# Reordering the attention work on VectorE, the loads of the last stage and the end of the block in a fused attention and gated-FFN kernel

## The chip, the cores and the metric

The kernel runs on one core of one Trainium2 chip. The metric is device time in microseconds (us) of one execution; lower is better.

## What is computed

`x` is layer-normalised once; the result feeds a local dilated attention (A) and a gated feed-forward network (B), and the output is `x + A * silu(B)`. There are 2048 tokens, 1024 features, 32 heads of 32, a window of 8 keys at a distance of 2, and 3584 hidden features.

```python
def reference(A_x, A_wqkv, A_wo, B_x, B_w1, B_w3, B_w2):
    xn = _layernorm(A_x)
    # attention: every query sees the keys at s, s-2, ..., s-14
    q, k, v = split(xn @ A_wqkv)                       # 32 heads of 32
    logits = einsum("bhsd,bhswd->bhsw", q, kg) * 32 ** -0.5
    attn = softmax(where(mask, logits, -1e9))
    s = einsum("bhsw,bhswd->bhsd", attn, vg) @ A_wo
    # gated FFN
    h = silu(xn @ B_w1) * (xn @ B_w3)
    g = silu(h @ B_w2)
    return A_x + s * g
```

## The kernel before

One function, `build`, writes a list of operations for each engine; an operation waits for those it depends on. Each engine, and each queue that issues transfers (SP's and POOL's), runs its list strictly in order. Four stages follow each other on TensorE (PE):

- **Normalisation and the first projection** (0 to about 45 us): rows are normalised on VectorE (DVE) and transposed on PE.
- **QKV projection** (to about 191 us): the 1024 features are cut into eight groups `g` of 128 (four heads). For each group and each of 16 row tiles PE makes 8 matmuls of 384 columns (L447), ScalarE (ACT) copies the result out and SP writes it to DRAM (`k_qkv_scr`). POOL's queue meanwhile loads the FFN's weights w3 and w1 (`k_w_sb`), a piece every four row tiles.
- **FFN** (to about 820 us): tokens are cut into eight blocks `b` of 256. An item S1(k) is 16 matmuls of 256 columns (L997) for one of 28 slices of hidden features; ACT then writes a sigmoid to `k_s_ring` (L1010) and a copy to `k_gu_ring` (L1012). Four items make a batch: two multiplications on DVE (L854, L855), `Hb_a` and `dH`. The ring holds 12 items, so ACT's L1010 of item k waits for the batch of item k-12. An item S3(k) is four matmuls of 512 columns (L1045), which need the batch of k and one 256 KB tile of w2. Segment `s` runs S1 of block s interleaved with S3 of block s-1: three S1 first, then pairs of one S3 and one S1, then three S3. Segment 0 has S1 only, segment 8 has S3 only. At the end of a segment ACT empties the accumulators (L1066 `aT2`, L1068 `aT2c`), POOL multiplies (L863, `dG`) and stores the gate `g` to DRAM (`gst`).
- **Final stage F** (to the end): for each of 16 row tiles the attention output is loaded (SP, `k_Or`), transposed on PE (L931, `pT`), multiplied with `wo` (L947, `pS`); DVE multiplies with `g` and adds `x` (L954, L956; their loads `k_gF` and `k_xF` come from POOL's queue), and POOL's queue stores the output.

The **attention** itself is done on DVE, in the gaps of its FFN work. For each group: **L**, eight steps of a product of q and k and a reduction (L561, L563); **S1**, mask, maximum and subtraction (three operations, to L583); the exponential `aE` on ACT; **S2**, sum, reciprocal and scaling (L603 to L605); **AV**, two halves of 8 steps (L623, L627, L629), each half followed by a store of `k_prod` to `k_O_scr` from POOL's queue (`Ost`). There is one buffer `k_prod`: the next L or AV half may start only when the store before it has landed. Q, K and V have one buffer each: loads for group g+1 are issued (POOL's queue) when the L, or the AV, of group g is done. `Er`, the output of `aE`, has two buffers, so `aE` of group g needs AV of group g-2.

What sets DVE's order is a planner in `build` that keeps estimated clocks for PE and DVE (`pe_clock`, `st["dv"]`). `advance_dve` picks, at each point of PE's list, the earlier of the next FFN batch and the next step of a fixed attention list `att_steps`: L(0), S1(0), L(1), S1(1), S2(0), AV(0), L(2), S1(2), S2(1), AV(1), and so on. The first two exponentials are put on ACT's list only where the FFN begins.

In segment 8 the w2 tiles go through six buffers, `w2r` (three), `w2tA` (two) and `w2tB` (one): tile k+6 is requested when S3(k) is done. Into SP's list between those requests the code puts one piece of `wo` at each even f from 2 and one load of the attention output at each odd f from 3, the latter with the two POOL loads of `g` and `x` (`F_loadgx`); one `pT` stands at f = 12, 16, 20 and 24.

```python
    with nc.Block() as block:                      # L98
...
    att_steps.append(("S2", g, 0, 0))              # L640, after L and S1 of group g+1
...
                if f >= 3 and f % 2 == 1 and ldO_left and F_can_loadO(ldO_left[0]):   # L976
```

## Time and profile before

| | us |
|---|---|
| median of 4 runs | 900.51 (897.93 to 904.2) |
| the profiled execution, its own time | 899.81 |
| span of its trace, first to last instruction | 898.0 |
| PE busy in the span | 836.5 |
| DVE busy | 631.1 |
| ACT busy | 329.1 |
| mean granted clock of PE | 0.975 of full |

The span and what lies around it (1.8 us) make the execution's own time. A busy figure is the time in which an engine has an instruction under way; matmuls overlap, so PE can be busy without running at its best rate. An idle time before an instruction carries a releaser: what ended it. Under `PEclk` stands the share of its full clock that PE was granted. Row numbers such as L997 are lines of the kernel before.

### The profile page before, as it was taken

The page shows a single profiled execution, that of the slowest core. Times are in us where ns is not written, and L with a number is a line of the kernel's source. Part 1 is how long each engine was busy: PE and PEld are TensorE (multiplying, and loading weights), DVE is VectorE, ACT ScalarE, POOL GpSimd, SP SyncE. Part 2 cuts the span into 40 slices and gives each one's busy share as a digit, 9 for nine tenths or more (in the row PEclk, how much of TensorE's full clock was granted, in tenths as well). Part 3 has the DMA queues.
Part 4 walks back from the last instruction along what each step waited for, and adds up shares of the span by engine and source line. Part 5 has one row for each costly group of instructions (what it writes and reads, how often), then busy time and mean ns, then how long its engine had stood idle before and what let it go on. Part 6 is the DMA issues. An engine that isn't in the chain of part 4 may idle for free.

```text
span 898.0 us, 14107 instructions
## 1 busy us (share of the span) xinstructions
PE 836.5 (93%) x5943; PEld 582.8 (65%) x6016; DVE 631.1 (70%) x624; ACT 329.1 (37%) x646; POOL 124.8 (14%) x170
## 2 busy tenths in 40 slices
PE   4999999999999999999998999899979999868995
PEld 3656665678877777777776776667657777523552
DVE  7558750047899879779978997997899797400553
ACT  3723233355533443453442343234224432402220
POOL 4322010000000020020002000100200020222341
PEclk9999999999999999999999899999989999978998
DMA  8288999730235465454545244454523454595772
GB/s 256 66 293 263 328 300 320 223 113 12 80 102 166 119 197 165 119 173 137 163 140 173 77 167 134 156 162 133 169 71 95 118 178 113 157 367 197 249 230 90
DMA packets 96176, 152.00 MB, mean 169 GB/s; under 512 B 32752, under 2 KB 52208, under 8 KB 96112
## 3 DMA queue, kind: packets, MB, share of 16 engines
q1 hardware_dynamic: 83072, 91.84, 34.3%
q0 software_dynamic: 13040, 59.25, 19.5%
q8 instruction: 47, 0.77, 0.3%
q14 instruction: 17, 0.14, 0.1%
HBM read 122.16 MB, written 28.90 MB: 168 GB/s over the span
## 4 chain that ended last, share of the span: by engine, by line
DVE 41%; PE 38%; DMA 10%; issue 7%; SPq 2%; ACT 1%; POOL 0%; DVEq 0%; POOLq 0%; ACTq 0%
PE k_ps L447 15%; DVE k_prod L627 11%; PE k_ps L997 9%; DVE k_Lr L563 7%; PE k_ps L1045 7%; DVE k_prod L561 7%; PE k_ps L947 6%; DVE k_prod L629 5%; DMA k_O_scr<-k_prod 5%; DVE k_s_ring L854 3%; DVE k_h_ring L855 3%; DMA k_qkv_scr<-k_ev 3%; SPq L84 2%; DMA k_w2tB<-in_B_w_dram 1%; DVE k_prod L623 1%
## 5 line engine op out<-in xcount | busy, mean ns | idle before, releaser
L997 PE MATMUL k_ps<-k_xblkB,k_w_sb 128*128 128x256 bf16 x1792 | 214.2, 274 | 5.8 <-ACT k_gu_ring L1012 5.8
L1010 ACT ACTIVATE k_s_ring<-k_ps 128x256 bf16<-128x256 f32 x224 | 88.1, 393 | 342.6 <-DVE k_h_ring L855 188.0
L1045 PE MATMUL k_ps<-k_w2r,k_h_ring 128*128 128x512 bf16 x781 | 203.2, 385 | 7.5 <-ACT k_accb L1068 3.8
L997 PEld LDWEIGHTS k_ps<-k_xblkB,k_w_sb 128*128 128x128 bf16 x1792 | 175.8, 98 | 49.8 <-ACT k_gu_ring L1012 8.0
L447 PE MATMUL k_ps<-k_wq,k_xnT_full 128*128 128x384 bf16 x1024 | 170.7, 328 | 5.8 <-DMA k_wq<-in_A_wqkv_dram 3.1
L997 PE MATMUL k_ps<-k_xblkA,k_w_sb 128*128 128x256 bf16 x1344 | 163.0, 276 | 12.0 <-ACT k_gu_ring L1012 12.0
L997 PEld LDWEIGHTS k_ps<-k_xblkA,k_w_sb 128*128 128x128 bf16 x1344 | 132.8, 99 | 46.7 <-ACT k_gu_ring L1012 14.0
L563 DVE TENSOR_REDUCE k_Lr<-k_prod 128x64 f32<-128x2048 bf16 x64 | 146.4, 2288 | 2.2
L447 PEld LDWEIGHTS k_ps<-k_wq,k_xnT_full 128*128 128x128 bf16 x1024 | 99.8, 98 | 71.7 <-issue 4.7
L627 DVE TENSOR_TENSOR k_prod<-k_Vb,k_Er 128x1024 bf16<-128x1024 bf16 x112 | 137.0, 1223 | 2.9
L1012 ACT ACTIVATE k_gu_ring<-k_ps 128x512 bf16<-128x512 f32 x224 | 136.2, 608 | 0.0
L1045 PEld LDWEIGHTS k_ps<-k_w2r,k_h_ring 128*128 128x128 bf16 x844 | 83.2, 99 | 67.4 <-issue 8.9
L561 DVE TENSOR_TENSOR k_prod<-k_Qb,k_Kb 128x2048 bf16<-128x2048 bf16 x64 | 87.4, 1365 | 50.7 <-DMA k_Kb<-k_qkv_scr 28.0
L453 ACT ACTIVATE k_ev<-k_ps 128x384 bf16<-128x384 f32 x128 | 57.8, 499 | 108.4 <-PE k_ps L447 54.6
L629 DVE TENSOR_TENSOR k_prod<-k_prod 128x1024 bf16<-128x1024 bf16 x112 | 77.5, 692 | 3.8
L954 DVE TENSOR_TENSOR k_gF<-k_ps,k_gF 128x1024 bf16<-128x1024 f32 x16 | 19.6, 1225 | 81.3 <-PE k_ps L947 81.3
L84 POOL DMA_DIRECT2D k_O_scr<-k_prod x16 | 14.5, 906 | 400.4 <-DVE k_prod L629 326.2
L947 PE MATMUL k_ps<-k_wo_sb,k_OTr 128*128 128x512 bf16 x249 | 59.7, 393 | 4.1 <-ACT k_accb L1068 3.7
L603 DVE TENSOR_REDUCE k_ss<-k_Er 128x64 f32<-128x512 bf16 x8 | 5.4, 679 | 67.8 <-ACT k_Er L590 67.8
L997 PE MATMUL k_ps<-k_xnT_full,k_w_sb 128*128 128x256 bf16 x448 | 49.1, 273 | 0.0
L997 PEld LDWEIGHTS k_ps<-k_xnT_full,k_w_sb 128*128 128x128 bf16 x448 | 43.8, 98 | 5.2
L947 PEld LDWEIGHTS k_ps<-k_wo_sb,k_OTr 128*128 128x128 bf16 x256 | 25.2, 101 | 33.5 <-ACT k_accb L1068 4.2
(51 smaller groups left out, 425.0 us busy)
## 6 DMA issues: line engine op xcount, KB each, us to landing
k_w2r<-in_B_w_dram SPq DMA_DIRECT2D x211, 256.0 KB, 2.6
k_w_sb<-in_B_w_dram POOLq DMA_DIRECT2D x16, 896.0 KB, 6.7
k_qkv_scr<-k_ev SPq DMA_DIRECT2D x32, 384.0 KB, 4.9
k_Kb<-k_qkv_scr POOLq DMA_DIRECT2D x8, 960.0 KB, 6.7
k_Vb<-k_qkv_scr POOLq DMA_DIRECT2D x8, 960.0 KB, 6.5
k_wq<-in_A_wqkv_dram SPq DMA_DIRECT2D x64, 96.0 KB, 5.3
k_x_in<-in_A_x_dram SPq DMA_DIRECT2D x8, 512.0 KB, 6.8
k_Qb<-k_qkv_scr POOLq DMA_DIRECT2D x8, 512.0 KB, 4.4
```

What stands on the lines that cost most here:

```text
L84: op.fns = [lambda e, o=out_ap, i=in_ap: e.dma_start(o, i)]
L447: fns = [lambda e, kt=kt, t=t, pos=pos, bk=bk: e.matmul(bank(bk, 0, NQ), lhsT=xnT_full[:, t // TB, kt, (t % TB) * P:(t % TB + 1) * P], rhs ...
L453: op_acB[idx] = AC.add(lambda e, idx=idx, bk=bk, pr=pr, t=t: e.activation(ev_ring[pr % 2][:, :, t % EVT_, :], bank(bk, 0, NQ).rearrange("p ...
L561: m = DV.add(lambda e, ksl=ksl: e.tensor_tensor(prodb[:], Qb[:], Kb[:, ksl:ksl + NT, :], ALU.mult), deps=deps, key=("Lm", g, w))
L563: last = DV.add(lambda e, w=w, g=g: e.tensor_reduce(Lview(Lr[0], w), prodb[:].rearrange("p t (h d) -> p (t h) d", d=DH), AX.X, ALU.add), d ...
L627: m = DV.add(lambda e, Vv=Vv, Pw=Pw: e.tensor_tensor(tmp, Vv, Pw, ALU.mult), deps=[AV_last[(g, hh)]], key=("AVm", g, hh, w))
L629: last = DV.add(lambda e: e.tensor_tensor(acc, acc, tmp, ALU.add), deps=[m], key=("AVa", g, hh, w))
L947: fns.append(lambda e, kt=kt, half=half, sl=sl, so=so: e.matmul(bank(4 + sl * ND + half, 0, 512), lhsT=OTr[so][:, kt, :], rhs=wo_sb[:, kt, ...
L997: fns.append(lambda e, kt=kt, f=f, b=b, k=k, which=which, wsb=wsb: e.matmul(bank(k % 4, which * NCOL, (which + 1) * NCOL), lhsT=wsb[:, kt, ...
L1010: AC.add(lambda e, k=k, sl=sl: e.activation(t_ring[:, sl, :], bank(k % 4, 0, NCOL), ACT.Sigmoid), deps=deps, key=("aS1t", k))
L1012: op_aS1[k] = AC.add(lambda e, k=k, sl=sl: e.activation(gu_ring[:, sl, :], bank(k % 4, 0, 2 * NCOL), ACT.Copy), deps=[op_pS1[k]], key=("aS ...
L1045: fns.append(lambda e, sub=sub, half=half, slot=slot, k=k, f=f, wbuf=wbuf: e.matmul(bank(4 + sub * ND + half, 0, 512), lhsT=h_ring[:, slot ...
```

## The change

Four things are changed.

1. The block is made with `no_gpsimd_drain=True`.
2. The one list of attention steps becomes two: `ls_steps` (L and S1) and `av_steps` (S2 and AV). At each point the planner may take the next step of either, whichever it estimates to start first (AV on a tie), but does not interrupt a group's L or AV. An L may start when S1 of the group before is in the list; four `Dr` buffers (`NDR`) bound how far L may run ahead of `aE`. The estimate also knows of the store of `k_prod` now (`ready_prod`, the end of the AV half plus 4.5 us).
3. `aE` of a group is put into ACT's list only when AV of the group two before stands in DVE's list, ahead of the batch that ACT waits for anyway.
4. In segment 8, the loads of two tiles of attention output and four pieces of `wo` are put into SP's list before the first tile request of the segment's own (k = 202), the other `wo` pieces at even f from 8; the four `pT` move from f = 12, 16, 20, 24 to f = 6, 8, 8, 12; the POOL loads of `g` and `x` are held back to f = 22 and wait for S3 of item 217.

```diff
-    with nc.Block() as block:
+    with nc.Block(no_gpsimd_drain=True) as block:
...
+        ready_prod[0] = st["dv"] + 4.5
...
+    def can_construct_exp(g):
+        return g in op_S1c and (g < 2 or (g - 2, NHALF - 1) in op_dAV)
...
-    for g in range(NG):
-        for w in range(W):
-            att_steps.append(("L", g, 0, w))
-        att_steps.append(("S1", g, 0, 0))
-        if g >= 1:
-            add_AV_steps(g - 1)
-    add_AV_steps(NG - 1)
+    for g in range(NG):
+        for w in range(W):
+            ls_steps.append(("L", g, 0, w))
+        ls_steps.append(("S1", g, 0, 0))
+        av_steps.append(("S2", g, 0, 0))
         for hh in range(NHALF):
             for w in range(W):
-                att_steps.append(("AV", g, hh, w))
+                av_steps.append(("AV", g, hh, w))
...
+    def next_att_step():
+        ls = ls_steps[ls_pos[0]] if ls_pos[0] < len(ls_steps) else None
+        av = av_steps[av_pos[0]] if av_pos[0] < len(av_steps) else None
+        ls_mid = ls is not None and (ls[0] == "S1" or (ls[0] == "L" and ls[3] > 0))
+        av_mid = av is not None and av[0] == "AV" and (av[3] > 0 or av[2] > 0)
+        cands = []
+        if av is not None and att_constructible(av) and not ls_mid:
+            cands.append((att_est_start(av), 0, "AV"))
+        if ls is not None and att_constructible(ls) and not av_mid:
+            cands.append((att_est_start(ls), 1, "LS"))
...
+            gx_hold[0] = True
+            for t_ in range(min(2, NT)):
+                if F_can_loadO(t_):
+                    F_loadO(t_)
...
+            construct_wo(0, 4)
+            wo_late = list(range(4, KT))
...
+                if f == 22:
+                    gx_hold[0] = False
+                    gx_dep.append(op_pS3[(s - 1) * FT + f - 1])
+                    for t_ in range(min(NFR, NT)):
+                        F_loadgx(t_)
+                    gx_dep.clear()
+                if f >= 8 and f % 2 == 0 and wo_late:
+                    k_ = wo_late.pop(0)
+                    construct_wo(k_, k_ + 1)
+                if f in (6, 8) and f_pref[0] < min(NOT_, NT):
...
-                if f >= 12 and f % 4 == 0 and f_pref[0] < min(NOT_, NT):
+                if f >= 8 and f % 4 == 0 and f_pref[0] < min(NOT_, NT):
```

How the lists change at three places. First, DVE's list at the end of S1(1) (its last operation writes `k_Dr`, L583 before, L585 after). Before:

```order
L577 TENSOR_TENSOR k_Lr_64<-k_Lr_64,k_Mmask_74 128x512
L580 TENSOR_REDUCE k_mx_23_71<-k_Lr_64 128x64
L583 TENSOR_TENSOR k_Dr_18_66<-k_Lr_64,k_mx_23_71 128x512
L603 TENSOR_REDUCE k_ss_24_72<-k_Er_19_67 128x64
L604 RECIPROCAL k_ss_24_72<-k_ss_24_72 128x64
L605 TENSOR_TENSOR k_Er_19_67<-k_Er_19_67,k_ss_24_72 128x512
L623 TENSOR_TENSOR k_prod_63<-k_Vb_62,k_Er_19_67 128x1024
```

The same engine and place after the change, with the end of L(2) and the start of L(3); `k_Qb`, `k_Kb` are the loaded queries and keys, `k_s_ring` and `k_h_ring` an FFN batch:

```order
L565 TENSOR_REDUCE k_Lr_64<-k_prod_63 128x64
L579 TENSOR_TENSOR k_Lr_64<-k_Lr_64,k_Mmask_74 128x512
L582 TENSOR_REDUCE k_mx_22_70<-k_Lr_64 128x64
L585 TENSOR_TENSOR k_Dr_28_76<-k_Lr_64,k_mx_22_70 128x512
L563 TENSOR_TENSOR k_prod_63<-k_Qb_60,k_Kb_61 128x2048
L565 TENSOR_REDUCE k_Lr_64<-k_prod_63 128x64
...
L882 TENSOR_TENSOR k_s_ring_57<-k_s_ring_57,k_gu_ring_58 128x1024
L883 TENSOR_TENSOR k_h_ring_59<-k_s_ring_57,k_gu_ring_58 128x1024
```

The whole of L(2), S1(2) and three steps of L(3) moved ahead of the first FFN batch and of S2(0). From there on L runs three groups ahead of AV: AV(0), L(4), AV(1), L(5), AV(2), L(6), AV(3), L(7), then AV(4) to AV(7) alone.

Second, SP's list in segment 8 from the last of the six first w2 tiles. Before (`k_Or` is a load of attention output):

```order
L84 DMA k_w2r_8_56<-in_B_w_dram 128x1024
L84 DMA k_w2r_6_54<-in_B_w_dram 128x1024
L84 DMA k_w2r_7_55<-in_B_w_dram 128x1024
L84 DMA k_wo_sb_83<-in_A_wo_dram 128x1024
L84 DMA k_w2r_8_56<-in_B_w_dram 128x1024
L84 DMA k_Or_36_84<-k_O_scr 128x1024
L84 DMA k_w2tA_58_106<-in_B_w_dram 128x1024
```

After:

```order
L84 DMA k_w2r_8_56<-in_B_w_dram 128x1024
L84 DMA k_Or_36_84<-k_O_scr 128x1024
L84 DMA k_Or_37_85<-k_O_scr 128x1024
L84 DMA k_wo_sb_83<-in_A_wo_dram 128x1024 x4
L84 DMA k_w2r_6_54<-in_B_w_dram 128x1024
L84 DMA k_Or_38_86<-k_O_scr 128x1024
L84 DMA k_w2r_7_55<-in_B_w_dram 128x1024
```

Six transfers of 256 KB stand ahead of the request for tile 202 (`k_w2r_6_54`), which stood directly behind tile 198 before.

Third, POOL's list in the FFN, after the last weight piece. Before:

```order
L84 DMA k_w_sb_81<-in_B_w_dram 128x3584 x6
L84 DMA k_O_scr<-k_prod_63 128x8x128 x2
L84 DMA k_Vb_62<-k_qkv_scr 128x3840
L84 DMA k_Qb_60<-k_qkv_scr 128x2048
L84 DMA k_Kb_61<-k_qkv_scr 128x3840
L84 DMA k_O_scr<-k_prod_63 128x8x128 x2
L84 DMA k_Vb_62<-k_qkv_scr 128x3840
L863 TENSOR_TENSOR k_t2gb_69<-k_t2gb_69,k_accb_79 128x2048
```

After, from the second pair of Q and K loads (group 4):

```order
L84 DMA k_Kb_61<-k_qkv_scr 128x3840
L84 DMA k_O_scr<-k_prod_63 128x8x128 x2
L84 DMA k_Vb_62<-k_qkv_scr 128x3840
L84 DMA k_Qb_60<-k_qkv_scr 128x2048
L84 DMA k_Kb_61<-k_qkv_scr 128x3840
L891 TENSOR_TENSOR k_t2gb_69<-k_t2gb_69,k_accb_79 128x2048
L84 DMA k_g_scr<-k_t2gb_69 128x2048
L84 DMA k_O_scr<-k_prod_63 128x8x128 x2
```

The stores of AV(1) now stand behind `dG` of block 0, which waits for the end of a segment; before they stood ahead of it.

## Rows read from the trace of the kernel before

**Rows 1.** The page: busy time, share and instructions of each engine.

```profile
PE 836.5 (93%) x5943; PEld 582.8 (65%) x6016; DVE 631.1 (70%) x624; ACT 329.1 (37%) x646; POOL 124.8 (14%) x170
```

**Rows 2.** Busy time by stretch: us; PE, PEld, DVE, ACT, POOL; PEclk, DMA share, GB/s.

```profile
240.00:412.00 172.00, 170.79 (x1304) 129.37 (x1324) 152.12 (x141) 70.51 (x142) 16.19 (x14) 1.00 0.50 151
412.00:661.00 249.00, 229.75 (x1696) 170.16 (x1723) 220.78 (x202) 90.86 (x190) 24.27 (x21) 0.97 0.46 142
775.00:821.00 46.00, 33.97 (x153) 14.70 (x154) 1.38 (x2) 9.09 (x9) 8.91 (x10) 0.85 0.89 310
821.00:898.00 77.00, 63.29 (x345) 31.05 (x352) 30.67 (x32) 15.44 (x14) 26.19 (x43) 0.91 0.52 172
```

**Rows 3.** Waits: engine, line, who is waited for; total us, times, longest.

```profile
PE k_ps L997 <- ACT k_gu_ring L1012: 17.8, 8, 6.1
ACT k_s_ring L1010 <- DVE k_h_ring L855: 188.0, 30, 13.6
DVE k_prod L623 <- DMA k_O_scr<-k_prod: 35.8, 8, 5.3
DVE k_prod L561 <- DMA k_O_scr<-k_prod: 21.3, 6, 4.3
```

**Rows 4.** Timeline of PE in the FFN: start, us, instruction, count, idle before.

```profile
191.44 48.74 PE L997 MATMUL k_ps<-k_xnT_full,k_w_sb 128*128 128x256 bf16 x445
...
754.82 1.91 PE L997 MATMUL k_ps<-k_xblkB,k_w_sb 128*128 128x256 bf16 x16
...
773.09 1.91 PE L997 MATMUL k_ps<-k_xblkB,k_w_sb 128*128 128x256 bf16 x16
```

**Rows 5.** Groups of DVE instructions: operands, count, busy us, mean ns, idle before.

```profile
L563 DVE TENSOR_REDUCE k_Lr<-k_prod 128x64 f32<-128x2048 bf16 x64 | 146.4, 2288 | 2.2
L627 DVE TENSOR_TENSOR k_prod<-k_Vb,k_Er 128x1024 bf16<-128x1024 bf16 x112 | 137.0, 1223 | 2.9
L561 DVE TENSOR_TENSOR k_prod<-k_Qb,k_Kb 128x2048 bf16<-128x2048 bf16 x64 | 87.4, 1365 | 50.7 <-DMA k_Kb<-k_qkv_scr 28.0 <-DMA k_O_scr<-k_prod 21.3
L629 DVE TENSOR_TENSOR k_prod<-k_prod 128x1024 bf16<-128x1024 bf16 x112 | 77.5, 692 | 3.8
L855 DVE TENSOR_TENSOR k_h_ring<-k_s_ring,k_gu_ring 128x1024 bf16<-128x1024 bf16 x56 | 38.7, 692 | 1.9
```

**Rows 6.** Timeline of DVE around the start of the FFN.

```profile
124.20 0.69 DVE L583 TENSOR_TENSOR k_Dr<-k_Lr,k_mx 128x512 f16<-128x512 f32 x1
192.68 0.69 DVE L603 TENSOR_REDUCE k_ss<-k_Er 128x64 f32<-128x512 bf16 x1 [67.79 <-ACT k_Er L590]
...
194.71 1.22 DVE L623 TENSOR_TENSOR k_prod<-k_Vb,k_Er 128x1024 bf16<-128x1024 bf16 x1
```

**Rows 7.** Timeline of POOL's queue: keys of group 2, last weight piece.

```profile
131.45 0.53 POOL L84 DMA_DIRECT2D k_Kb<-k_qkv_scr  x1
...
163.30 0.53 POOL L84 DMA_DIRECT2D k_w_sb<-in_B_w_dram  x1 [4.67 <-PE k_ps L447]
```

**Rows 8.** DMA issues by tile: count, KB each, median us to landing.

```profile
k_Kb<-k_qkv_scr POOLq DMA_DIRECT2D x8, 960.0 KB, 6.7
```

**Rows 9.** Timeline of PE in segment 8 and at the start of stage F.

```profile
781.41 4.44 PE L1045 MATMUL k_ps<-k_w2r,k_h_ring 128*128 128x512 bf16 x12 [3.83 <-ACT k_accb L1068]
...
798.75 1.89 PE L1045 MATMUL k_ps<-k_w2tA,k_h_ring 128*128 128x512 bf16 x4 [4.94 <-DMA k_w2tA<-in_B_w_dram]
...
824.22 6.50 PE L947 MATMUL k_ps<-k_wo_sb,k_OTr 128*128 128x512 bf16 x16 [3.74 <-ACT k_accb L1068]
```

**Rows 10.** The chain that ended last, in segment 8: start, us, what.

```profile
789.32 12.28 DMA k_w2tB<-in_B_w_dram
```

**Rows 11.** Busy time by stretch, as in Rows 2, inside segment 8.

```profile
780.00:790.00 10.00, 8.53 (x31) 3.44 (x32) 0.00 (x0) 1.27 (x1) 8.35 (x9) 0.83 0.68 214
790.00:800.00 10.00, 3.48 (x12) 1.06 (x12) 0.00 (x0) 0.00 (x0) 0.56 (x2) 0.80 1.01 376
```

**Rows 12.** Line 98, the block's end, by queue: duration ns, start us.

```profile
L98 POOLq DRAIN  x1: 5221/5221/5221, 892.6 to 892.6; - x1
```

More of the change, by code (lines that the diff above doesn't have):

```diff
@@ L502, in build @@
     prod_users = []
+    ready_prod = [0.0]
     op_group_ready = {}
@@ L699, in do_att_step, with take_att_step, att_done @@
                     try_pending_loads()
+    def next_att_step():
[8 more added lines that the diff above has]
+            cands.append((att_est_start(ls), 1, "LS"))
+        if not cands:
+            return None
+        cands.sort()
+        return cands[0]
+    def take_att_step(which):
+        if which == "AV":
+            step = av_steps[av_pos[0]]; av_pos[0] += 1
+        else:
+            step = ls_steps[ls_pos[0]]; ls_pos[0] += 1
+        do_att_step(step)
+    def att_done():
+        return av_pos[0] >= len(av_steps) and ls_pos[0] >= len(ls_steps)
     ffn_q = []
@@ L814, in build @@
     in_ffn[0] = True
-    while exp_pending:
+    while exp_pending and can_construct_exp(exp_pending[0]):
         g_ = exp_pending.pop(0)
@@ L868, in build, with construct_wo @@
     KEY_OST_ALL = (NG - 1, NHALF - 1)
-    def construct_wo():
+    def construct_wo(k0=0, k1=KT):
         nonlocal op_wo
-        for kt in range(KT):
+        for kt in range(k0, k1):
             op_wo = SP.dma(wo_sb[:, kt, :], A_wo[kt * P:(kt + 1) * P, :], s_wo,
@@ L1080, in build @@
     flush_act_deferred(pe_clock[0], force=True)
-    while exp_pending:
+    while exp_pending and can_construct_exp(exp_pending[0]):
         g_ = exp_pending.pop(0)
@@ L1085, in build @@
     guard = 0
-    while att_pos[0] < len(att_steps) or ffn_q:
+    while (not att_done()) or ffn_q:
         guard += 1
-        assert guard < 100000, (att_pos[0], len(att_steps), len(ffn_q))
-        before = (att_pos[0], len(ffn_q))
+        assert guard < 100000, (ls_pos[0], av_pos[0], len(ffn_q))
+        before = (ls_pos[0], av_pos[0], len(ffn_q))
         advance_dve(st["dv"] + 50.0)
         flush_act_deferred(st["dv"], force=True)
-        while exp_pending:
+        while exp_pending and can_construct_exp(exp_pending[0]):
             g_ = exp_pending.pop(0)
@@ L1096, in build @@
         try_pending_loads()
-        if (att_pos[0], len(ffn_q)) == before and att_pos[0] < len(att_steps):
-            step = att_steps[att_pos[0]]
-            assert att_constructible(step), f"attention step {step} not constructible at end"
+        if (ls_pos[0], av_pos[0], len(ffn_q)) == before and not att_done():
+            assert False, ("attention scheduling stuck", ls_pos[0], av_pos[0])
     T_ATT_END = st["dv"]
```

72 lines of the change are left out of this document (36 added, 36 removed).

## The prediction, written before the changed kernel had run

> **What bounds the kernel now.** I read the busy times first. PE is busy 93% of the span and DVE 70% [rows 1], so the end is set by PE's list plus what PE waits for, and the question is where PE waits. The table by stretch answers that [rows 2]: from 240 to 412 us PE loses next to nothing, from 412 to 661 it is busy 230 of 249 us at a granted clock of 0.97, and in segment 8 (775 to 821) only 34 of 46 us at 0.85. The waits give the two reasons. In the FFN, S1 items wait for ACT's copy (17.8 us, 8 times), and ACT for DVE's batch (188.0 us) [rows 3]: DVE is the pace-setter there. In segment 8 PE waits for w2 tiles [rows 9, 10].
>
> How much is lost? PE's undisturbed pace stands in its timeline: 28 items S1 in 48.74 us, 1.74 each, and a pair of S1 and S3 every (773.09 - 754.82) / 7 = 2.61 us, so 0.87 for an S3 [rows 4]. Segment 0 starts at 191.44; seven segments of 28 pairs (73.1 each) follow, and the last three S3 stand behind the last S1. Undisturbed, the last S1 would end at 191.44 + 48.74 + 511.6 - 2.6 = 749.2. It ended at 773.09 + 1.75 = 774.8. The FFN thus loses **25.6 us**: 17.8 of waits, and 3% of the 249 us, 7.5, at the reduced clock around them [rows 2, 3].
>
> Why is DVE late? One group of attention costs it, by mean durations [rows 5]: L 8 x (1.365 + 2.288) = 29.2, AV 16 x 1.223 + 14 x 0.692 = 29.3, S1 and S2 about 2.0 each (S2 runs from 192.68 to 194.71 [rows 6]; S1 has three operations too and is priced alike); 62.6 together. A batch is two operations of 0.69, 1.4. In the old order 36 batches stand in the five groups from L(2) to L(7), 7.2 per group, 10.1 us; and two waits for the store of `k_prod`, 35.8 / 8 = 4.5 and 21.3 / 6 = 3.6 [rows 3]. Sum 80.8 us per group, against 7.2 x 4 x 2.61 = 75.2 on PE: 5.6 too much, 28 over five groups, which is the loss found above. Meanwhile DVE stood idle for 67.8 us in the QKV stage, from the end of S1(1) at 124.9 until the first exponential [rows 6].
>
> **The change, part by part.** *Attention order (edits 2 and 3).* L(2), S1(2) and three steps of L(3) move into that idle time. K of group 2 is requested at 131.45 as before [rows 7] and lands 6.7 us later [rows 8]; L(2) and S1(2) then take DVE to about 170. The request for group 3 follows the end of L(2) and the last weight piece (163.30 [rows 7]), and lands at about 175; three steps of 3.65 end near 186. The first batch is ready at about 191.4 + 4 x 1.74 + 1 = 199.4 (the 1 is ACT's two copies, 0.5 each by its 329.1 us for 646 instructions [rows 1]), so DVE waits for it and is not late. The cost on the QKV stage is one more pair of Q and K loads while PE still runs; I take 0, since PE there needs only what was asked for long before; if the stores of q, k, v were held up by one such load, it would be up to 6.7.
>
> Now DVE's sum against PE's, stretch by stretch. Batch 0 to 9: five steps of L(3) 18.3, S1 and two S2 6.1, AV(0) 29.3, nine batches 12.6, one store wait 4.5: 70.8. PE needs for those batches 24 items at 1.74, then three S1 and nine pairs: 41.8 - 1 + 5.2 + 23.5 = about 70. Even. From the start of L(4) (behind batch 9) to that of L(7) (behind batch 32) stand three groups and 23 batches: 187.8 + 32.2 = 220.0. The store wait after a first half is up to 4.5, and in two of three groups a batch of 1.4 stands in it: 10.7. The wait after a second half (3.6) now has S2 and a batch (3.4) ahead of the next L: 0.6. Gaps between instructions: DVE is idle 28.2 us in 412 to 661 [rows 2], of which store waits are about 3.06 x 8.1 = 24.8, so 3.4. Sum **234.7**, against 23 x 10.44 = **240.1** on PE. Last, AV(5) to AV(7) have no L beside them, so each must wait for its V load: 8 us (6.7 by the K load of the same size [rows 8] and the issues ahead). 3 x (29.3 + 2 + 4.5 + 8) + 15 x 1.4 = 152.4, against 15 x 10.44 = 156.6. DVE is therefore almost full, but no longer over-full; and a late batch j is only missed 9 items later (ring of 12), 9 x 2.61 = 23.5 us. So PE should hardly wait: I take the whole loss back, **25.5 us**, with 13 as the low end (the first rival). The last S1 then ends near 749, and AV(7), six operations behind batch 53, near 740. New on POOL's queue: stores now stand behind `dG`, which waits for a segment's end; I take 0 (the slow rival).
>
> *Segment 8 (edit 4).* Before, S3 ran from 781.41 to 820.5 (824.22 - 3.74), 39.1 us [rows 9]. At its pace it needs 28 x 0.87 = 24.4, four transposes of 8 x 128 columns 4 x 0.45 = 1.8 (half the columns of an S1's 16 matmuls per matmul, 8 of them), and the slow start after the wait for ACT, 4.44 for 12 matmuls instead of 2.6 [rows 9], 1.8: 28.0. So 11.1 us go to late w2 tiles and the clock after them; PE waited 4.94 for one of them [rows 9], and another, asked for at 789.32, took 12.28 to be used [rows 10]. In that time the queues were full, 376 GB/s at a DMA share of 1.01, after only 214 GB/s in the ten microseconds before [rows 11]. Until S3 ends, 28 + 8 + 4 tiles of 256 KB on SP's queue, 8 of POOL's `g` and `x` loads and 2 for the store of `g` had to move, 13.1 MB or 35 us at 376 GB/s; holding back `g` and `x` leaves 42 tiles, 11.0 MB, 29 us. Six tiles now go out in the first half-empty microseconds. Is tile 202 late behind them? It is asked for when S3(196) is done, about 6.6 + 1.5 = 8.1 us after the last S1; the 12 tiles ahead need 8.4 us at 376 GB/s, so it lands at 12 to 13, and PE wants it at 6.6 + 4.4 + 3 x 0.87 + 0.4 = 14.0. Just in time. I leave 1.6 us of waits and take **9.5 us**; ends 3 (tile 202 exposed and the clock low again) and 11.1.
>
> The Trainium skill, "DMA: Bandwidth & Descriptors", section "Queues, rings and completion order", states that each engine takes a queue's descriptors in ring order. It speaks against this edit: by it tile 202 lands only after all six tiles put ahead of it. [rows 10] fit it but cannot separate it from the full queues. If the 1.57 MB came out of PE's time in full, the sum would be 4.2 us worse; that is the second rival, worked out below from the rows.
>
> The `g` and `x` loads issued at f = 22 take eight issues of 0.53 and one landing, about 11 us; DVE wants the first after the remaining 6 x 0.87, the 3.74 wait and the first `pS` of 6.50 [rows 9], 15.5 us. Hidden, with 4 us to spare. Stage F keeps its 77 us [rows 2].
>
> *End of the block (edit 1).* After the last store POOL's queue runs a DRAIN of 5.22 us, from 892.6 to 897.8, and the span ends at 898.0 [rows 12]. Nothing else runs. I take **5.2**; it is 0 if the same work is done after the span.
>
> **Sum.** 25.5 + 9.5 + 5.2 = 40.2. The profiled execution took 899.81, 0.7 less than the median of 900.51, so 859.6 for it and 860.3 for the median: I say 860. Its own range: 22 to 25.6, 7 to 11.1, 5.1 to 5.3 give 34 to 42, so 858.5 to 866.5, and some 3 us of spread between runs.
>
> **Rivals.**
> - *DVE still sets the pace.* If its groups cost as much over PE's pace as before, 5.6 us, because the store waits stay exposed, six groups are 34 us, of which the ring absorbs 23.5. The last S1 is 10 to 13 late: **872**. For: my sum has 5 us to spare in 240. Against: two of the six store waits per three groups are now covered by work that stands in the list.
> - *Segment 8 gives little.* The queue moves tiles no faster; tile 202 comes 4.2 us late and the clock falls again, so 3 remain of 9.5: **866.5**. For: 11.0 MB need 29 of the 36 us even at the best rate. Against: the rate before was 214 GB/s where the six tiles now go.
> - *The drain comes back outside the span:* **865**.
> - *Slower than before.* AV's stores queue on POOL behind `dG`, which waits for PE's segment; DVE cannot go on without the store, and PE's batches stand behind it on DVE. Place: the first half of AV(1) to AV(5). By list position `dG` of block 0 is free about 4 us before its store is wanted, that of block 4 about when it is. With X us lost at each of five, 5X - 23.5 reaches PE; above X = 13 the gain is gone, and at X = 15 the time is **912**. Nothing in the trace shows such a wait yet.
>
> **How the numbers follow.** The forecast 0.64; DVE 0.10; segment 8 0.12; drain 0.09; slower 0.02; the rest, gains that cancel to within 0.5% (about what a measurement of this kernel can tell from no change), 0.03. Faster 0.95, same 0.03, slower 0.02. The range runs from the largest gain of every term and a fast run, 855, to the first rival, 873.
>
> **What would show it.** Right: PE's waits for `k_gu_ring` near 0; DVE's idle before the first S2 cut from 68 us to a wait of some 13 before the first batch; last S1 near 749; S3 of segment 8 in about 29.5 us; nothing behind the last memset. Wrong: waits of L1010 for batches that still reach PE; PE waiting for tile 202 or the first transpose; `k_O_scr` stores issued right behind `dG`; an own time that is not shorter by what the span is.

## The result, and the profile after

The changed kernel takes **863.66 us** (median of 10 runs, 859.58 to 868.38) against 901.4 of the kernel before on the same chip: ratio **0.9579, 95% interval 0.9559 to 0.9599**. A second set of runs gave 862.38 and 0.9546 (0.9525 to 0.9566). The forecast was 860, between 855 and 873. The profiled execution took 863.72 us with a span of 861.9, so what lies around the span is 1.8 us, as before.

The page's first line (the answer to [rows 1]) shows PE busy 8 us less than before, in a span that is 36 us shorter; nothing was taken out of PE's work, it waits less and runs less often at a reduced clock:

```profile
PE 828.5 (96%) x5943; PEld 580.1 (67%) x6016; DVE 638.4 (74%) x624; ACT 336.1 (39%) x646; POOL 127.6 (15%) x170
```

Busy time by stretch, in the columns of [rows 2]. The stretch 412 to 661 had PE busy 229.75 of 249 us at 0.97; now it is 247.27 at 1.00. Segment 8 lies between 753 and 790; its last 30 us run at 350 GB/s and a DMA share of 0.98:

```profile
412.00:661.00 249.00, 247.27 (x1879) 186.47 (x1908) 216.91 (x215) 102.52 (x205) 26.30 (x20) 1.00 0.48 144
760.00:790.00 30.00, 28.54 (x141) 12.67 (x142) 0.00 (x0) 3.98 (x4) 8.34 (x10) 0.92 0.98 350
790.00:862.00 72.00, 62.91 (x346) 30.92 (x352) 30.65 (x32) 15.92 (x14) 26.19 (x43) 0.94 0.63 212
```

The waits (columns of [rows 3]). All of PE's waits behind the QKV stage stand here, and the one for `k_gu_ring` (17.8 us, 8 times) is not among them. On DVE the waits for the store of `k_prod` fell from 35.8 and 21.3 us to 13.3 and 2.7, and DVE now waits 19 times for a batch, 61.9 us in all. It is early:

```profile
PE k_ps L1093 <- DMA k_w2r<-in_B_w_dram: 6.1, 5, 3.9
PE k_ps L978 <- ACT k_accb L1116: 3.7, 1, 3.7
PE k_ps L1093 <- DMA k_w2tA<-in_B_w_dram: 0.5, 1, 0.5
...
DVE k_s_ring L882 <- ACT k_gu_ring L1059: 61.9, 19, 12.5
DVE k_prod L628 <- DMA k_O_scr<-k_prod: 13.3, 5, 3.9
DVE k_prod L563 <- DMA k_O_scr<-k_prod: 2.7, 3, 1.2
```

In the kernel before that same wait of DVE was found once:

```profile
DVE k_s_ring L854 <- ACT k_gu_ring L1012: 4.2, 1, 4.2
```

PE's timeline gives the places at which the time is split: the start of the FFN, the last S1, the first S3 of segment 8, the first `pS`:

```profile
192.95 3.22 PE L1043 MATMUL k_ps<-k_xnT_full,k_w_sb 128*128 128x256 bf16 x28
...
751.17 1.91 PE L1043 MATMUL k_ps<-k_xblkB,k_w_sb 128*128 128x256 bf16 x16
...
759.52 5.24 PE L1093 MATMUL k_ps<-k_w2r,k_h_ring 128*128 128x512 bf16 x12 [3.86 <-DMA k_w2r<-in_B_w_dram]
...
793.84 6.02 PE L978 MATMUL k_ps<-k_wo_sb,k_OTr 128*128 128x512 bf16 x16 [3.74 <-ACT k_accb L1116]
```

Against [rows 4, 9], with the last S1 ending 1.75 us after its start and the last S3 of segment 8 ending 3.74 us ahead of the first `pS`:

| stretch | before | after | gained | forecast |
|---|---|---|---|---|
| start to first S1 | 191.44 | 192.95 | -1.5 | 0, at worst -6.7 |
| first S1 to end of last S1 | 583.4 | 560.0 | 23.4 | 25.5 |
| to the end of S3 in segment 8 | 45.6 | 37.2 | 8.5 | 9.5 |
| to the end of the span | 77.6 | 71.8 | 5.7 | 5.2 |
| span | 898.0 | 861.9 | 36.1 | 40.2 |

### The profile page after: what moved, and what is told of

Read it like the earlier page. It is cut to its first block, busy times and chain, and to the rows that moved or that the text cites. A ratio compares the mean times of both kernels' runs of the same rounds, so it can differ in the third digit from the quotient of the medians.

```text
span 861.9 us, 14095 instructions
## 1 busy us (share of the span) xinstructions
PE 828.5 (96%) x5943; PEld 580.1 (67%) x6016; DVE 638.4 (74%) x624; ACT 336.1 (39%) x646; POOL 127.6 (15%) x170
## 3 DMA queue, kind: packets, MB, share of 16 engines
q1 hardware_dynamic: 83072, 91.84, 35.8%
## 4 chain that ended last, share of the span: by engine, by line
PE 89%; DMA 7%; SPq 2%; issue 1%; ACT 1%; DVE 0%; POOL 0%; POOLq 0%; ACTq 0%
PE k_ps L1043 44%; PE k_ps L1093 21%; PE k_ps L447 16%; PE k_ps L978 6%; DMA k_qkv_scr<-k_ev 3%; DMA k_w2r<-in_B_w_dram 3%; SPq L84 2%; PE k_ps L962 1%; PE k_ps L469 1%; DMA k_wq<-in_A_wqkv_dram 1%; DMA k_w2tA<-in_B_w_dram 1%; DMA out_dram<-k_ob 0%; ACT k_t2gb L1114 0%; ACT k_accb L1116 0%; DVE k_gF L985 0%
## 5 line engine op out<-in xcount | busy, mean ns | idle before, releaser
L1057 ACT ACTIVATE k_s_ring<-k_ps 128x256 bf16<-128x256 f32 x224 | 86.1, 384 | 311.1 <-PE k_ps L1043 310.8
L447 PE MATMUL k_ps<-k_wq,k_xnT_full 128*128 128x384 bf16 x1024 | 172.6, 330 | 5.4 <-ACT k_ev L453 3.4
L1043 PE MATMUL k_ps<-k_xblkA,k_w_sb 128*128 128x256 bf16 x1344 | 159.4, 273 | 0.0
L632 DVE TENSOR_TENSOR k_prod<-k_Vb,k_Er 128x1024 bf16<-128x1024 bf16 x112 | 144.6, 1291 | 3.1
L1059 ACT ACTIVATE k_gu_ring<-k_ps 128x512 bf16<-128x512 f32 x224 | 133.2, 594 | 0.0
L563 DVE TENSOR_TENSOR k_prod<-k_Qb,k_Kb 128x2048 bf16<-128x2048 bf16 x64 | 79.7, 1246 | 54.3 <-DMA k_Kb<-k_qkv_scr 50.1
L634 DVE TENSOR_TENSOR k_prod<-k_prod 128x1024 bf16<-128x1024 bf16 x112 | 85.0, 759 | 3.8
L882 DVE TENSOR_TENSOR k_s_ring<-k_s_ring,k_gu_ring 128x1024 bf16<-128x1024 bf16 x56 | 38.4, 687 | 62.0 <-ACT k_gu_ring L1059 61.9
L891 POOL TENSOR_TENSOR k_t2gb<-k_t2gb,k_accb 128x2048 bf16<-128x2048 bf16 x8 | 35.4, 4426 | 139.9 <-ACT k_accb L1116 139.9
L84 POOL DMA_DIRECT2D k_O_scr<-k_prod x16 | 14.4, 902 | 280.7 <-DVE k_prod L634 259.1
L1043 PE MATMUL k_ps<-k_xnT_full,k_w_sb 128*128 128x256 bf16 x448 | 49.1, 273 | 0.0
```

The source lines that it names most:

```text
L447: fns = [lambda e, kt=kt, t=t, pos=pos, bk=bk: e.matmul(bank(bk, 0, NQ), lhsT=xnT_full[:, t // TB, kt, (t % TB) * P:(t % TB + 1) * P], rhs ...
L563: m = DV.add(lambda e, ksl=ksl: e.tensor_tensor(prodb[:], Qb[:], Kb[:, ksl:ksl + NT, :], ALU.mult), deps=deps, key=("Lm", g, w))
L632: m = DV.add(lambda e, Vv=Vv, Pw=Pw: e.tensor_tensor(tmp, Vv, Pw, ALU.mult), deps=[AV_last[(g, hh)]], key=("AVm", g, hh, w))
L634: last = DV.add(lambda e: e.tensor_tensor(acc, acc, tmp, ALU.add), deps=[m], key=("AVa", g, hh, w))
L882: a = DV.add(lambda e: e.tensor_tensor(tv, tv, gv, ALU.mult), deps=deps, key=("Hb_a", j))
L1043: fns.append(lambda e, kt=kt, f=f, b=b, k=k, which=which, wsb=wsb: e.matmul(bank(k % 4, which * NCOL, (which + 1) * NCOL), lhsT=wsb[:, kt, ...
```

## The experiments

The theory: three separate gains, of the end of the block (edit 1), of segment 8 (edit 4) and of DVE's order in the FFN (edits 2 and 3, which were only tried together); inside the last, work that moves into DVE's idle time before the FFN, and stores that are covered by batches. The rivals are the prediction's: DVE still sets the pace, segment 8 gives little, the drain comes back outside the span, stores wait behind `dG`. The first three runs take the edits apart, the others go into them. The place of the last S1 is given here by the start of its last matmul: 774.73 in the kernel before, 752.80 in the changed one; the first `pS` follows 49.5 and 41.0 us later. Line numbers in rows are those of the kernel that ran.

**The end of the block alone.**

```diff
-    with nc.Block() as block:
+    with nc.Block(no_gpsimd_drain=True) as block:
```

> The kernel before with edit 1 alone (no drain at the block's end). If the 5.22 us DRAIN was plain waiting: 5.2 us shorter than before, ratio 0.994, span end right behind the last memset. If the work moves behind the span: the span is 5.2 us shorter, the own time is not, ratio 1.000, and own time minus span grows from 1.8 to about 7 us.

896.68 us, 0.994 (0.9922 to 0.9959). The row of [rows 12] has no counterpart in its trace. What POOL's queue still does at that line, in the same view (duration ns, start us), are two semaphore events; the other queues keep their own drains, of which the last to start takes 0.73 us:

```profile
L98 POOLq EVENT_SEMAPHORE  x2: 17/17/17, 894.5 to 894.6; - x2
L98 DVEq DRAIN  x1: 730/730/730, 891.1 to 891.1; - x1
```

So the 5.22 us are gained in the span, and the time around it stays 1.8: the drain doesn't come back outside.

**The attention order alone** (edits 2 and 3 on the kernel before).

> The kernel before with the new attention order (edits 2 and 3) alone; old loads in segment 8, old end. Theory: the last S1 ends near 753 instead of 775, 22 us shorter, segment 8 keeps about 45.6 us from last S1 to last S3; about 879, ratio 0.975. Rival (the order brings little, the loads in segment 8 were what counted): within 5 us of before.

877.51 us, 0.9724 (0.9702 to 0.9745). No S1 waits for the ring; the last S1 is at 755.00, and from there to the first `pS` it takes 49.1 us, as without the change. The rival in which DVE still sets the pace falls.

**Segment 8 alone** (edit 4 on the kernel before).

> The kernel before with the new loads of segment 8 (edit 4) alone. Theory: the last S1 still ends near 775, the way from there to the last S3 falls from 45.6 to about 37 us; 8.5 us shorter, ratio 0.9905. Rival (the gain there needs the earlier end of attention, since the first loads of attention output wait for AV(7)): 3 us or less.

894.56 us, 0.9907 (0.9879 to 0.9935). PE's waits for `k_gu_ring` are all there (21.1 us, 9 times), those for w2 tiles in segment 8 shrink to 0.7 us in all, and the last S1 (778.13) is followed by the first `pS` after 39.6 us, ten less than before. The rival in which segment 8 gives little falls. The three parts gain 0.6%, 2.8% and 0.9%, 4.3% together; the whole change gains 4.2%. Within their intervals they add up, and each shows without the others.

**Without the early L.** L(2) and what follows stay behind S2(0), as before; the rest of the change stands.

```diff
-            return g in op_Qld and (g == 0 or (g - 1) in op_S1c)
+            return g in op_Qld and (g == 0 or (g - 1) in op_S1c) and (g < 2 or 0 in op_S2c)
```

> The changed kernel, with L(2) and all later L put behind S2(0) in DVE's list, so that DVE idles in the QKV stage as before; the two lists, the planner's knowledge of stores, the loads and the end stay as changed. Theory (moving 42 us of L into the idle time is the gain): DVE is over-full again, S1 items wait for batches, the last S1 ends 15 to 30 us later than in the changed kernel, and AV(7) ends so late that the first transposes of segment 8 wait too; 880 to 895. Rival (the freer order and the covered store waits are the gain): the last S1 within 5 us of 753, 862 to 868.

882.61 us, 0.9778 (0.9749 to 0.9807). The loss, 19 us against the changed kernel, is as large as was expected, but it stands in another place. PE waits for no batch and the last S1 is at 752.93, as in the changed kernel. What is late is the attention: the last store of AV(7) goes out at 767.70 instead of 740.68, and in segment 8 PE waits for the loads of its output. The waits of PE and of DVE:

```profile
PE k_ps L962 <- DMA k_Or<-k_O_scr: 15.2, 4, 7.4
...
DVE k_ss L608 <- ACT k_Er L595: 71.0, 1, 71.0
```

and the last store of AV(7) in the timeline of POOL's queue:

```profile
767.70 0.90 POOL L84 DMA_DIRECT2D k_O_scr<-k_prod  x1 [3.19 <-DVE k_prod L634]
```

DVE has its 71.0 us of idle time ahead of the FFN back. So the early L is not what makes the batches punctual; it lets AV(7) end before the last S1. The theory was changed here: the batches are punctual because the planner puts more of them ahead of each group, and the early L pays for the attention that this delays. The next two runs test it.

**The planner's estimate of the store alone.** On the kernel before, only `ready_prod`: the one list of steps, no early L.

```diff
+        ready_prod[0] = st["dv"] + 4.5
...
-            return max(st["dv"], ready_Q.get(g, 1e9))
+            return max(st["dv"], ready_Q.get(g, 1e9), ready_prod[0])
```

(and the same for both halves of AV)

> The kernel before (one list, old loads, old end) in which only the planner's estimate knows of the store of k_prod (the end of the AV half plus 4.5 us). The list then has 8 batches per group instead of 7.2, 83.5 us of PE for the 81 us that DVE needs. Theory formed after e4 (how many batches stand among a group's steps sets PE's pace, not how much work lies in the idle time): no waits of S1 items, the last S1 near 753 to 755; but half of AV(7) stands behind the last batch, its store lands near 770 to 780, and segment 8 waits for it: 20 us or more from the last S1 to the first transposes, total 880 to 890. Rival (DVE's total work in the FFN is what counts): S1 waits as before, the last S1 at 770 to 778, 895 to 903.

893.12 us, 0.9897 (0.987 to 0.9923). No S1 waits, and the last S1 is at 751.97: this one estimate of the planner removes the whole loss that the prediction found in the FFN. The stores are as exposed on DVE as before (33.8 and 24.5 us, against 35.8 and 21.3). What changed is the order: the planner thinks that an L or AV starts later, and puts a batch ahead of it, so there are 8 batches per group of attention instead of 7.2, and the lateness goes to the attention. AV(7) is stored at 804.43, and PE stands still for its load between segment 8 and stage F (PE's timeline):

```profile
814.75 1.03 PE L935 MATMUL k_ps<-k_ident,k_Or 128*128 128x128 bf16 x8 [22.39 <-DMA k_Or<-k_O_scr]
```

The store is 24 us later than the upper end of what was expected, the time 3 us above it.

**The change without that estimate.**

```diff
-        ready_prod[0] = st["dv"] + 4.5
```

> The changed kernel without that estimate: early L, two lists, new loads and end as changed. From L(4) to L(7) stand 21 batches instead of 23, 219 us of PE for about 231 of DVE; the lag adds up to some 37 us by AV(7), of which the ring absorbs 23.5. Theory (density of batches sets the pace): S1 items wait late in the FFN, the last S1 8 to 15 us later than in the changed kernel, 870 to 878. Rival (the 42 us of L in the idle time are enough room): the last S1 within 3 us of 753, 861 to 866.

869.22 us, 0.9632 (0.9612 to 0.9653). AV(7) is stored early, at 735.41, but now batches are late: PE waits for three of them, and the last S1 is at 759.62, 6.8 us behind the changed kernel, a little less than expected. Waits of PE and DVE:

```profile
PE k_ps L1042 <- ACT k_gu_ring L1058: 6.4, 3, 4.1
...
DVE k_prod L627 <- DMA k_O_scr<-k_prod: 34.0, 8, 5.6
```

The store waits of the AV halves are back at 34.0 us. With the estimate they are 13.3 in the changed kernel and 21.3 in the run without early L: it covers a part of them, and more where the early L leave other work to put there.

How late a batch is can be read from its two neighbours, the end of ACT's fourth copy and the start of its first multiplication. For the 21st batch of the kernel before they stand in the timeline of ACT:

```profile
384.68 0.59 ACT L1012 ACTIVATE k_gu_ring<-k_ps 128x512 bf16<-128x512 f32 x1
```

and in that of DVE:

```profile
409.94 0.68 DVE L854 TENSOR_TENSOR k_s_ring<-k_s_ring,k_gu_ring 128x1024 bf16<-128x1024 bf16 x1
```

For the changed kernel, ACT's timeline again:

```profile
387.44 0.59 ACT L1059 ACTIVATE k_gu_ring<-k_ps 128x512 bf16<-128x512 f32 x1
```

and DVE's:

```profile
389.01 0.68 DVE L882 TENSOR_TENSOR k_s_ring<-k_s_ring,k_gu_ring 128x1024 bf16<-128x1024 bf16 x1
```

24.7 us before, 1.0 after. Over all 56 batches the same reading grows from 0.3 to 24.7 in the kernel before and stays between 21 and 37 up to the 53rd; in the changed kernel it is never above 4.7, in the run without early L never above 10.6, with the estimate alone never above 16.4, and without the estimate it grows to 31.0. The prediction's figure for when PE notices was 23.5, and of these five kernels the two in which S1 waits are the two that pass it. The figure was a little low: in these two, every S1 item that waits over half a microsecond waits for a batch that is 27.5 to 37.4 us late.

**More work on DVE.** The changed kernel with nine more row sums per group.

```diff
+        for _ in range(9):
+            a = DV.add(lambda e, g=g: e.tensor_reduce(ssb[g % 2][:], E3, AX.X, ALU.add), deps=[a], key=("S2x", g))
```

> The changed kernel with nine more copies of the row sum ahead of every S2 on DVE (their result is the same; 0.68 us each, 6.1 us per group of attention, 6 groups within the FFN). DVE's list is otherwise unchanged. It asks how much room DVE has left in the FFN. Theory of the prediction (DVE almost full, 234.7 of 240.1 us between L(4) and L(7); a batch that is late by up to 23.5 us isn't missed by PE): batches fall behind by 6.1 per group less the little room, 15 to 30 us by batch 50 and about 5 of that reach PE at most; last S1 at 753 to 758; AV(7) is stored 12 to 25 us later, near 755 to 765, so the first transposes of segment 8 may wait for their loads; a time of 866 to 877. Rival 1 (no ring slack: every us of DVE comes out): 6 x 6.1 = 37 us, about 895 to 900. Rival 2 (DVE has more room than the prediction's sum says): last S1 and AV(7) within 3 us of the changed kernel, 863 to 866.

875.43 us, 0.9659 (0.9612 to 0.9707). Three of the four executions took 875 to 877 us, the fourth 866.52; the trace is of the longest, 877.34. The batches fall up to 32 us behind, the last S1 is at 761.55, and PE's wait for the ring is back among its waits:

```profile
PE k_ps L1095 <- DMA k_w2r<-in_B_w_dram: 10.1, 6, 4.0
...
PE k_ps L1045 <- ACT k_gu_ring L1061: 7.2, 4, 2.7
```

The last store of AV(7) goes out 24 us later than in the changed kernel (POOL's queue):

```profile
764.60 0.89 POOL L84 DMA_DIRECT2D k_O_scr<-k_prod  x1 [19.58 <-DVE k_prod L636]
```

All eight S2 stand within the FFN, not six, so DVE got 49 us more, not 37. They came out as 8.7 us at the last S1 (3.5 beyond what was expected) and 13 at the end. Most of the rest came out of DVE's waits for batches, which fell from 61.9 to 14.4 us; the ring allows that, since a batch may be late. So DVE has little room between L(4) and L(7), where the prediction's sum put it, and more behind L(7).

The part that is lost in segment 8 shows how its loads hang on the attention: the early loads of attention output wait on SP for the last store of AV(7), and the request for tile 202 stands behind them. It goes out at 772.64, 11.1 us after the last S1 instead of 8.6, and PE waits for it (PE's timeline):

```profile
779.25 1.89 PE L1095 MATMUL k_ps<-k_w2r,k_h_ring 128*128 128x512 bf16 x4 [3.51 <-DMA k_w2r<-in_B_w_dram]
```

**Without holding back `g` and `x`.**

```diff
-            gx_hold[0] = True
+            gx_hold[0] = False
```

> The changed kernel with the loads of g and x issued as before, right behind the store of g, not held back to f = 22. If the hold is what pays in segment 8: PE waits for w2 tiles by 5 to 9 us again, the way from the last S1 to the last S3 grows from 37 to 42 to 46 us; 868 to 872. If the early wo and attention loads are what pays: within 2 us of the changed kernel.

871.32 us, 0.9654 (0.9634 to 0.9673). From the last S1 to the first `pS` it takes 45.6 us instead of 41.0. The eight loads go out between 768.5 and 772.8, and in the ten us behind them PE has 6.5 us of work, at 0.69 of its clock, with the queues full (columns of [rows 2]):

```profile
775.00:785.00 10.00, 6.50 (x24) 2.63 (x24) 0.00 (x0) 1.47 (x2) 0.00 (x0) 0.69 1.04 389
```

The rest of the difference stands ahead of segment 8: this execution began its FFN at 196.75, 3.8 us later, although its list is the same there. The changed kernel's own two traces differ by 1.9 us at that place (192.95 and 191.04), but the four executions of this run agree within 1.4 us, so a shift of one execution need not be all of it. How much of the 7.7 us between the medians is the hold's beyond those 4.6 stays open.

**`wo` as before**, a piece at every even f from 2, the rest of the change as it is.

```diff
-            construct_wo(0, 4)
-            wo_late = list(range(4, KT))
+            wo_late = list(range(KT))
...
-                if f >= 8 and f % 2 == 0 and wo_late:
+                if f >= 2 and f % 2 == 0 and wo_late:
```

> The changed kernel with the eight pieces of wo at even f from 2 as before; the two early loads of attention output, the early transposes and the hold stay. If the early wo pieces are what pays: 3 us or more longer. If they cost tile 202 its place in the queue: its wait (3.9 us in the changed kernel's trace) goes and the time is up to 4 us shorter. If they change nothing: within 2 us.

864.59 us, 0.958 (0.9557 to 0.9603): no difference. The 3.9 us that the expectation lays on tile 202 are the wait of the first S3 for its own tile (k = 196); tile 202 was used without a wait. That first S3 comes 6.7 us after the last S1 in both, released by its w2 tile in the changed kernel and by ACT here, as in the changed kernel's second trace:

```profile
758.51 1.87 PE L1092 MATMUL k_ps<-k_w2r,k_h_ring 128*128 128x512 bf16 x4 [3.83 <-ACT k_accb L1115]
```

**Two tries at something faster**, beside a second set of runs of the changed kernel.

> The changed kernel once more, beside the next two on one chip, so that they can be set against it as well as against the kernel before. Both theories: ratio to before 0.956 to 0.960, last S1 at 752 to 755 us, first pS at 793 to 796, span 861 to 864.

862.38 us, 0.9546 (0.9525 to 0.9566), just under what was expected; last S1 at 750.93, first `pS` 41.4 us later.

The first try empties the accumulators of the last two segments in two halves, so that `pS` and the first S3 can start after the first half:

```diff
-            op_aT2[b] = AC.add(lambda e: e.activation(t2gb[:].rearrange("p a d -> p (a d)"), accv, ACT.Sigmoid),
...
+                for a_ in range(TB):
+                    accs = ps[:, ACC_LO + a_ * D: ACC_LO + (a_ + 1) * D]
+                    op_aT2[b] = AC.add(lambda e, a_=a_, accs=accs: e.activation(t2gb[:, a_, :], accs, ACT.Sigmoid),
...
+                    op_aT2c[b] = AC.add(lambda e, a_=a_, accs=accs: e.activation(accb[:, a_, :], accs, ACT.Copy),
```

> The changed kernel with the evacuation of PE's accumulators in two halves at the last two block ends (per half a sigmoid and a copy of 1024 columns instead of one of each over 2048), so that the first four S3 of segment 8 and the first pS start after the first half. In the changed kernel PE waits 3.74 us for ACT before the first pS and as long, or for its w2 tile, before the first S3 of segment 8 (3.86). Theory (after the FFN the path runs through PE, its waits for ACT and w2, so a wait taken away there comes out at the end): the wait before the first pS falls to about 2.0 us (two operations of about 1.0), the one before the first S3 too unless the w2 tile that is waited for there is late by itself (then it stays about 3.8), and the clock falls less: 2 to 4.5 us less than the changed kernel, a time of 859 to 862, ratio 0.953 to 0.956. Rival (stage F is paced by its loads, its sums on DVE or its stores): pS starts earlier and the span ends where it ended, ratio 0.957 to 0.959.

861.12 us, 0.9536 (0.9514 to 0.9558). The interval overlaps that of the changed kernel: no difference that these runs can tell, and the 2 to 4.5 us of the theory are not shown. In the trace, the wait ahead of the first `pS` falls from 3.74 to 2.03 and the 16 matmuls behind it take 3.63 us instead of 6.02; but the first S3 waits longer, for its tile:

```profile
760.02 2.72 PE L1098 MATMUL k_ps<-k_w2r,k_h_ring 128*128 128x512 bf16 x6 [4.65 <-DMA k_w2r<-in_B_w_dram]
...
792.41 3.63 PE L979 MATMUL k_ps<-k_wo_sb,k_OTr 128*128 128x512 bf16 x16 [2.03 <-ACT k_accb L1139]
```

The second gives the first three tiles of segment 8 the buffers that are free 2.6 us earlier:

```diff
-    w2t = list(w2r) + [sb(f"w2tA{i}", [P, D], BF16, i * 2 * KB) for i in range(2)] \
-        + [sb(f"w2tB{i}", [P, D], BF16, xb_addr + i * 2 * KB) for i in range(2)]
+    w2t = [sb(f"w2tA{i}", [P, D], BF16, i * 2 * KB) for i in range(2)] \
+        + [sb("w2tB0", [P, D], BF16, xb_addr)] + list(w2r)
...
```

> The kernel of e10_half_evacuation, and the last segment takes its w2 tiles from the three buffers that are free at the last S1 first (w2tA, w2tA, w2tB), then from the three of the ring that become free with the last S3 of segment 7. In e10_half_evacuation the first S3 of segment 8 waited 4.65 us for a ring tile that was asked for at 755.39, 2.9 us after the last S1, because its buffer was in use until then, and landed at 760.0; a tile in w2tA is asked for 2.6 us earlier. Theory (that wait is the reuse of the buffer): first S3 about 5 us after the last S1 instead of 7.5, 2 to 3 us less than e10_half_evacuation until the first pS or less where later tiles then wait for the full queues, first pS 37.5 to 39.5 us after the last S1 (39.9 in e10_half_evacuation, 41.0 to 41.4 in the changed kernel), a time of 858 to 861, ratio 0.950 to 0.954. Rival (segment 8 is paced by the bytes that its tiles bring): the first S3 starts earlier and the later S3 wait for it, first pS 39.5 to 41 us after the last S1, ratio as before, 0.953 to 0.956.

861.84 us, 0.954 (0.9516 to 0.9565). The first S3 does start 5.0 us after the last S1 instead of 7.5, released by ACT (PE's timeline):

```profile
759.92 1.23 PE L1098 MATMUL k_ps<-k_w2tA,k_h_ring 128*128 128x512 bf16 x4 [2.12 <-ACT k_accb L1139]
```

Six later ones wait 5.1 us for ring tiles instead, where it was 1.3 (PE's waits):

```profile
PE k_ps L1107 <- DMA k_w2r<-in_B_w_dram: 5.1, 6, 2.0
```

From the last S1 to the first `pS` it takes 39.3 us, against 39.9 and 41.0: at the edge of what the theory allowed, while time and ratio are the rival's. Of the 2.5 us gained at the first S3, 0.6 are left at the first `pS`. That speaks for a segment 8 paced by the bytes of its tiles by now; it is one trace of each. No version was found that beats the changed kernel measurably.

## Why the prediction was right, and where it was not

The forecast of 860 is 3.7 us under the median; its range holds it. By its steps:

- **FFN, 25.5 forecast, 23.4 measured.** The place was right (waits for the ring and the clock around them), and so was the undisturbed pace: first S1 to last S1 was to take 557.8 us and took 560.0. The 2.2 are a wait of 1.4 for a w2 tile and PE's gaps.
- **The sum for DVE** between the start of L(4) and that of L(7) was 234.7 us. DVE's timeline has the two starts,

```profile
274.71 1.23 DVE L563 TENSOR_TENSOR k_prod<-k_Qb,k_Kb 128x2048 bf16<-128x2048 bf16 x1 [0.98 <-DMA k_O_scr<-k_prod]
...
515.86 1.23 DVE L563 TENSOR_TENSOR k_prod<-k_Qb,k_Kb 128x2048 bf16<-128x2048 bf16 x1 [0.50 <-DMA k_O_scr<-k_prod]
```

  and the window between them (us, DVE busy, PEclk, DMA share, GB/s) is

```profile
274.71:515.86 241.15, 221.01 (x203) 1.00 0.50 151
```

  241.15 us, of which 5.5 are waits for batches (5 times): 235.6 of DVE's own time, and 241.15 against PE's 240.1. Store waits in it are 10.5, forecast 11.3. The sum was good to a microsecond, and with it the statement that DVE is nearly full there. In part that is luck: three operations in this window were held by POOL (last section) and took 8.9 us more than usual, where the prices of the prediction held 3.3.
- **The old loss**, 28 us worked out for five groups against 25.6 found, agreed by luck. By the ring's 23.5, which the prediction counts on in the new order, 28 us of lateness would have cost PE only 4.5. The price of a group was right (81.0 us from the start of L(2) to that of L(7), 80.8 forecast), but DVE fell behind by more than the sum has: the 42nd batch is 37.4 us late, and PE is by then 15 us behind its own undisturbed pace, 52 together. Less a slack of some 27, that is the loss. One part that the sum lacks: the first of the 36 batches still come at the pace of segment 0, where PE needs 1.74 us for an item, not 2.61. DVE's two starts in the kernel before:

```profile
239.08 1.23 DVE L561 TENSOR_TENSOR k_prod<-k_Qb,k_Kb 128x2048 bf16<-128x2048 bf16 x1 [3.74 <-DMA k_O_scr<-k_prod]
...
643.99 3.19 DVE L561 TENSOR_TENSOR k_prod<-k_Qb,k_Kb 128x2048 bf16<-128x2048 bf16 x1 [2.74 <-DMA k_O_scr<-k_prod]
```

- **AV(5) to AV(7)** were priced with 8 us each for their V loads. There was no wait for `k_Vb` at all, and from the start of L(7) to the last batch DVE waited 38.1 us for batches. The step was too dear by 24 us, without effect, since PE set the pace there. AV(7) ended where it was to: its last store goes out at 740.68, forecast near 740.
- **What the terms rest on** is where the reasoning falls short of the runs. The prediction took the gain in the FFN from two things at once, attention moved ahead of the FFN and more batches per group, and gave no share to either. The runs separate them. More batches per group alone (the estimate alone, or the change without early L) make S1 free of waits. But then the attention ends at 768 (without early L) or 804 (the estimate alone), and PE pays for it in segment 8 or right behind it, 15 and 23 us. The early L pays for that. Which of the two lists is late is the planner's choice; that both are punctual takes the moved work. In the prediction AV(7) "near 740" stands as a remark, and it is a condition.
- **QKV stage, 0 taken, -1.5 measured**, inside the bounds given, and not an effect of the change. The last stretch of it starts at the same time and takes 43.44 us instead of 41.76; in PE's timeline the kernel before has

```profile
149.84 41.76 PE L447 MATMUL k_ps<-k_wq,k_xnT_full 128*128 128x384 bf16 x256 [1.62 <-ACT k_ev L453]
```

  and the changed one

```profile
149.67 43.44 PE L447 MATMUL k_ps<-k_wq,k_xnT_full 128*128 128x384 bf16 x256 [2.13 <-ACT k_ev L453]
```

  In the table by stretch PE's granted clock from 125 to 191 is 0.97 instead of 1.00, behind that wait for ACT, which is 0.5 longer. The other traces settle whose effect this is. The second trace of the changed kernel has the shorter time, behind a longer wait:

```profile
149.45 41.76 PE L447 MATMUL k_ps<-k_wq,k_xnT_full 128*128 128x384 bf16 x256 [2.37 <-ACT k_ev L453]
```

  and the run of the end alone, whose lists up to here are those of the kernel before, has the longer one:

```profile
150.62 43.44 PE L447 MATMUL k_ps<-k_wq,k_xnT_full 128*128 128x384 bf16 x256 [2.21 <-ACT k_ev L453]
```

  From 145 to 160 us the granted clock is 0.89 in the two traces with 43.44 and 1.00 in the two with 41.76. So the early L cost the QKV stage nothing that shows, as the prediction took it, and the 1.5 is chance.
- **Segment 8, 9.5 forecast, 8.5 measured**, S3 in 30.6 us (29.5 forecast). Two of three arguments held: `g` and `x` out of the way are worth some 4.6 us there, and tile 202 comes in time (asked for at 761.42, landed at 766.02, used at 767.63 without a wait, 14.7 after the last S1, forecast 14.0). Of the third, six early tiles that fill half-empty microseconds, four were tested and gave nothing that could be measured. Without the hold, 45.6 of 49.5 us are left from the last S1 to the first `pS`; which part of the edit gains these 3.9 us (the two early loads of attention output, the earlier transposes) no run separates. Not foreseen was the wait of the first S3 for its own tile, whose buffer is free only with the last S3 of segment 7; it costs nothing as long as ACT takes equally long.
- **The rule of the Trainium skill** on the order within a queue ("DMA: Bandwidth & Descriptors", "Queues, rings and completion order") would have cost 4.2 us here if the tiles ahead had delayed tile 202 past its use. The rule is about the order in which descriptors, the pieces of a transfer, are taken; that the tile also lands behind all six is what the trace shows (the last of the six at 765.33, tile 202 at 766.02). With four of the six taken away from there it landed 2.7 us after its request instead of 4.6, and the time did not change: it was there before it was wanted in either order. The run with more work on DVE, where it is asked for later, is the case in which PE waits for it.
- **End, 5.2 forecast**, 5.7 with the first `pS` a little faster (6.02 instead of 6.50). Right.
- **The slow rival**, stores behind `dG` on POOL's queue, exists and costs nothing: one store in the changed kernel follows the store of `g` at once (692.15), 0.4 us after its half of AV had ended, where a store that follows nothing takes 0.3.

The missing 4.1 us of the sum are thus 1.5 in the QKV stage, which are chance, 2.1 in the FFN and 1.0 in segment 8, less 0.5 at the end.

## What to carry to other kernels

Where one engine serves two consumers from one list, ask of a new order which consumer it makes late, and follow that one to where it is waited for; a wait that disappears from the profile may only have changed its customer. The idle time of an engine ahead of a stage was worth something here because the end of the moved work, the attention's last store, is on the path later. Where a stage moves bytes at a full queue, starting it earlier may give waits back later.
